# A spectral-filter and gated-MLP layer rewritten: one-instruction GELU, a stacked 64x32 FFT with trips through DRAM, and another order of work

## The chip, the cores and the metric

The kernel runs on one core of one Trainium2 chip. Times are device microseconds (us) of one execution. A quoted time is the median of several executions, with the lowest and highest behind it. Engines: PE is TensorE's matmul stream and PEld its weight loads, DVE is VectorE, ACT is ScalarE, POOL is GpSimd, SP is SyncE, which issues DMAs here (in the kernel before, ScalarE issues a part of them). An eviction is the copy of a matmul's result out of PSUM, where TensorE writes it. A DMA's landing is its end as the profile shows it. The chain of waits is the work that ended last, followed back from the end of the execution: at each step to what released it.

## The reference

```python
# x: (1, 2048, 576), hidden width Fh = 2304, everything in bfloat16
xn = layernorm(x)
# branch A: a spectral filter over both axes
s  = irfft2(rfft2(xn) * (w_r + 1j * w_i))
# branch B: a gated MLP that mixes over the 2048 rows
z  = gelu(xn @ w_in)                       # 2048 x 4608, the tanh form of GELU
z1, z2 = z[:, :2304], layernorm(z[:, 2304:])
g  = w_sp @ z2 + b_sp[:, None]             # w_sp: 2048 x 2048
out = x + s * silu((z1 * g) @ w_out)       # w_out: 2304 x 576
```

## The kernel before

It works in four stages: normalise all rows of x; compute z2 (for 16 row tiles) while the FFT of branch A runs between; mix over rows, one group of 128 hidden columns at a time (18 groups, all 2048 rows each); multiply by `w_out` and finish. Three parts matter here.

GELU was spelled out, two ScalarE passes and four VectorE passes for each tile:

```python
def gelu_from_psum(ph, nsz, dst, pp):                                    # L265
    nc.scalar.activation(out=hs, in_=ph, func=ACT.Identity)              # L267
    nc.vector.tensor_tensor(out=x2t, in0=hs, in1=hs, op=ALU.mult)        # L269
    nc.vector.tensor_scalar(out=x2t, in0=x2t, scalar1=GELU_K, scalar2=1.0, ...)   # L270
    nc.vector.tensor_tensor(out=ut, in0=x2t, in1=hs, op=ALU.mult)        # L273
    nc.scalar.activation(out=sg, in_=ut, func=ACT.Sigmoid, scale=GELU_S2)  # L275
    nc.vector.tensor_tensor(out=dst, in0=hs, in1=sg, op=ALU.mult)        # L276
```

(slices of the tiles are left out). The z2 loop (L476 to L493) makes each row of z2 with it, takes statistics, and stores the row to DRAM, from where the main loop loads it back by columns and normalises it.

The FFT over the 2048 rows was 128 x 16, with real and imaginary parts in separate matmuls and TensorE transposes between the steps. Four of its loops transpose; one of the two that also multiply, with matmuls of 128 columns:

```python
for lq in range(LQ):                                                     # L398, 37 times
    for c in range(2):
        nc.tensor.transpose(pt[:], Ev[:, c, lq, :], ident[:])
        nc.any.tensor_copy(out=dtt[:, c, :], in_=pt[:])
    nc.tensor.matmul(pvr[:], lhsT=H[:, 0, :], rhs=dtt[:, 0, :], start=True, stop=False)
    nc.tensor.matmul(pvr[:], lhsT=H[:, 2, :], rhs=dtt[:, 1, :], start=False, stop=True)
    nc.tensor.matmul(pvi[:], lhsT=H[:, 0, :], rhs=dtt[:, 1, :], start=True, stop=False)
    nc.tensor.matmul(pvi[:], lhsT=H[:, 1, :], rhs=dtt[:, 0, :], start=False, stop=True)
    nc.any.tensor_copy(...)   # two more evictions of 128x128
```

The main loop (L543 to L582) makes z1 for a group (L561, GELU), then multiplies `z2t` by all of `w_sp` (L571).

## Time and profile before

The kernel takes 760.86 us (759.58 to 761.64, 5 runs). The stages, read from the timeline and the groups by line:

| stretch, us | what runs | what bounds it |
|---|---|---|
| 0 to 36 | normalisation of x | VectorE and the loads |
| 36 to 187 | z2, with FFT steps between | VectorE |
| 187 to 348 | the rest of the FFT, alone | a chain of short matmuls and evictions |
| 348 to 676 | z1 and the mixing over rows | TensorE |
| 676 to 759 | load of `w_out`, output | TensorE, after a wait |

From parts 1 and 2 of the page of the kernel before. Each digit is the busy share of one fortieth of the span in tenths; PEclk is the granted TensorE clock in tenths.

```profile
PE 672.2 (89%) x3638; PEld 341.6 (45%) x3638; DVE 522.8 (69%) x1598; ACT 332.8 (44%) x900; POOL 15.7 (2%) x32
PE   3599977878795896797999999999999999989997
DVE  7779999998879533215987777777777778642322
PEclk9999999898556555598999999999999999999999
```

The 89% for TensorE hides three different limits (slices counted from 0). From slice 19 on PE is at 9 nearly throughout. In slices 3 to 8 DVE is at 9. In slices 10 to 16 no engine stays there, and the clock is at 5 or 6.

The busy time of each engine by stretch, kernel before. The columns after the stretch and its length are busy us and instructions of PE, PEld, DVE, ACT and POOL, then the granted clock, the DMA share and GB/s.

```profile
57.00:190.00 133.00, 110.99 (x578) 59.69 (x576) 128.07 (x403) 99.91 (x252) 0.42 (x2) 0.92 0.16 64
190.00:323.00 133.00, 104.23 (x608) 63.76 (x609) 72.68 (x219) 91.41 (x351) 7.19 (x4) 0.54 0.35 69
348.00:676.00 328.00, 328.00 (x1509) 148.18 (x1510) 253.25 (x736) 86.05 (x145) 3.08 (x15) 0.99 0.16 37
```

In the first line VectorE is busy 128 of 133 us: it is the bound. In the second no engine is busy throughout, and TensorE's 104 busy us are at a clock of 0.54. In the third TensorE is busy all 328 us. VectorE is busy 253 us there too, but nobody waits for it for long.

The GELU groups of the kernel before, by form. Columns: line, engine, operation, tiles, sizes, count, then busy us and mean ns of one.

```profile
L267 ACT ACTIVATE hs<-ph 128x512 bf16<-128x512 f32 x136 | 80.1, 598 | 205.9 <-PE ph L561 183.6 <-PE pf L285 10.0 <-DVE zrow L276 6.5
L269 DVE TENSOR_TENSOR x2t<-hs 128x512 bf16<-128x512 bf16 x136 | 56.2, 414 | 27.5 <-ACT hs L267 27.5
L270 DVE TENSOR_SCALAR x2t<-x2t 128x512 bf16<-128x512 bf16 x136 | 37.9, 288 | 0.8
L273 DVE TENSOR_TENSOR ut<-x2t,hs 128x512 bf16<-128x512 bf16 x136 | 55.7, 419 | 0.1
L275 ACT ACTIVATE sg<-ut 128x512 bf16<-128x512 bf16 x136 | 84.0, 630 | 61.1 <-DVE ut L273 36.0 <-DMA wb<-in_B_w_in_dram 24.5
L276 DVE TENSOR_TENSOR zrow<-hs,sg 128x512 bf16<-128x512 bf16 x64 | 26.4, 417 | 3.1 <-ACT sg L275 3.0
```

A 512-wide tile costs VectorE 414 + 288 + 419 + 417 = 1,538 ns. TensorE needs five matmuls of 216 ns for it, 1,080 ns. So in the z2 loop VectorE must set the pace.

A piece of the chain of waits of the kernel before (start us, us, what):

```profile
429.91 11.22 PE pg L571 x52
```

11.22 us by 52 is 215.8 ns for a 512-wide matmul in a dense stream.

### The profile page before, as it was taken

How to read it: one execution, taken by the hardware profiler on the slowest of the kernel's cores; microseconds unless marked ns; L12 is line 12 of the kernel's file. 1: busy time of each engine (PE TensorE's matmuls, PEld its weight loads, DVE VectorE, ACT ScalarE, POOL GpSimd, SP SyncE). 2: the span in 40 equal slices, each digit the busy share in tenths (PEclk: the TensorE clock that was granted, in tenths of full speed). 3: DMA queues.
4: the chain of work that ended last, by engine and by line, in shares of the span. 5: the costliest groups of instructions: out<-in, count | busy, mean ns of one | idle time of the engine just before them, and what ended most of it. 6: DMA issues, size and time to landing. Idle time of an engine off the chain costs nothing.

```text
span 759.1 us, 10654 instructions
## 1 busy us (share of the span) xinstructions
PE 672.2 (89%) x3638; PEld 341.6 (45%) x3638; DVE 522.8 (69%) x1598; ACT 332.8 (44%) x900; POOL 15.7 (2%) x32
## 2 busy tenths in 40 slices
PE   3599977878795896797999999999999999989997
PEld 1276533333562563353444444444444444434553
DVE  7779999998879533215987777777777778642322
ACT  3447787677774677734222222222222223202222
POOL 2000000000000110000000000000000000000000
PEclk9999999898556555598999999999999999999999
DMA  7091111111598000034311111111111210025331
GB/s 265 18 315 71 63 63 62 64 62 63 124 217 135 1 1 0 1 104 115 84 38 35 37 36 36 36 37 36 36 37 44 48 43 1 0 90 169 95 109 56
DMA packets 104374, 54.08 MB, mean 71 GB/s; under 512 B 84160, under 2 KB 101184, under 8 KB 104192
## 3 DMA queue, kind: packets, MB, share of 16 engines
q10 hardware_dynamic: 61040, 29.36, 13.6%
q1 hardware_dynamic: 43280, 24.05, 12.1%
q8 instruction: 28, 0.46, 0.2%
q14 instruction: 26, 0.21, 0.1%
HBM read 30.85 MB, written 14.16 MB: 59 GB/s over the span
## 4 chain that ended last, share of the span: by engine, by line
PE 70%; DVE 17%; ACT 8%; issue 2%; DMA 2%; ACTq 0%; DVEq 0%
PE pg L571 33%; PE ph L561 11%; PE py L600 9%; PE ph L485 5%; DVE stats L490 4%; PE py L461 3%; DVE zrow L276 2%; DVE x2t L269 2%; DVE ut L273 2%; PE pt L435 2%; ACT G L438 2%; DVE x2t L270 1%; ACT dtt L406 1%; PE pvr L410 1%; PE pxr L346 1%
## 5 line engine op out<-in xcount | busy, mean ns | idle before, releaser
L571 PE MATMUL pg<-WSPT,z2t 128*128 128x512 bf16 x1152 | 253.9, 379 | 0.0
L267 ACT ACTIVATE hs<-ph 128x512 bf16<-128x512 f32 (+1 forms) x152 | 85.6, 577 | 205.9 <-PE ph L561 183.6
L571 PEld LDWEIGHTS <-z2t 128*128 128x128 bf16 x1152 | 112.7, 98 | 136.0
L275 ACT ACTIVATE sg<-ut 128x512 bf16<-128x512 bf16 (+1 forms) x152 | 89.0, 607 | 61.3 <-DVE ut L273 36.2
L485 PE MATMUL ph<-WIN,xnT 128*128 128x512 bf16 (+1 forms) x400 | 96.1, 389 | 7.0 <-ACT hs L267 6.4
L561 PE MATMUL ph<-xnT,wb 128*128 128x512 bf16 x360 | 85.3, 387 | 4.9 <-DMA wb<-in_B_w_in_dram 4.9
L577 DVE TENSOR_TENSOR BUF<-pg,z1T 128x512 bf16<-128x512 f32 x72 | 49.5, 688 | 44.5 <-PE pg L571 43.7
L269 DVE TENSOR_TENSOR x2t<-hs 128x512 bf16<-128x512 bf16 (+1 forms) x152 | 60.0, 400 | 27.5 <-ACT hs L267 27.5
L600 PE MATMUL py<-WOUT,BUF 128*128 128x512 bf16 (+1 forms) x576 | 73.0, 289 | 3.9 <-DMA WOUT<-in_B_w_out_dram 3.7
L554 DVE TENSOR_SCALAR z2t<-z2t,RSTD,NMR 128x128 bf16<-128x128 bf16 x288 | 74.0, 312 | 1.8 <-DMA z2t<-z2n_d 1.5
L485 PEld LDWEIGHTS <-xnT 128*128 128x128 bf16 x400 | 40.8, 104 | 52.0 <-issue 26.6
L273 DVE TENSOR_TENSOR ut<-x2t,hs 128x512 bf16<-128x512 bf16 (+1 forms) x152 | 59.0, 405 | 0.1
L561 PEld LDWEIGHTS <-wb 128*128 128x128 bf16 x360 | 35.8, 100 | 48.9 <-issue 7.9
L600 PEld LDWEIGHTS <-BUF 128*128 128x128 bf16 x576 | 37.4, 99 | 40.0 <-issue 6.3
L490 DVE BATCH_NORM_STATS2 stats<-zrow 128x6 f32<-128x384 bf16 x96 | 48.2, 548 | 0.0
L606 DVE TENSOR_TENSOR g<-hx,sgm 128x576 bf16<-128x576 bf16 x16 | 7.3, 458 | 55.1 <-ACT sgm L604 44.2
L603 ACT ACTIVATE hx<-py 128x512 bf16<-128x512 f32 (+1 forms) x32 | 13.2, 414 | 66.7 <-PE py L600 46.1
L270 DVE TENSOR_SCALAR x2t<-x2t 128x512 bf16<-128x512 bf16 (+1 forms) x152 | 40.1, 281 | 0.8
L197 PE MATMUL pt<-ident,xn 128*128 128x128 bf16 (+1 forms) x80 | 14.2, 296 | 21.4 <-DVE xn L192 18.9
L276 DVE TENSOR_TENSOR zrow<-hs,sg 128x512 bf16<-128x512 bf16 (+1 forms) x80 | 29.7, 391 | 3.1 <-ACT sg L275 3.0
L276 DVE TENSOR_TENSOR z1T<-hs,sg 128x512 bf16<-128x512 bf16 x72 | 30.1, 419 | 1.9 <-ACT sg L275 1.5
L580 DVE TENSOR_TENSOR BUF<-BUF,zb 128x512 bf16<-128x512 bf16 x72 | 29.0, 422 | 1.3
(131 smaller groups left out, 736.0 us busy)
## 6 DMA issues: line engine op xcount, KB each, us to landing
z2t<-z2n_d ACTq DMA_DIRECT2D x18, 512.0 KB, 3.9
z2n_d<-zrow ACTq DMA_DIRECT2D x8, 576.0 KB, 2.8
z2n_d<-zrow SPq DMA_DIRECT2D x8, 576.0 KB, 2.8
sspec_d<-srow ACTq DMA_DIRECT2D x16, 144.0 KB, 1.8
wb<-in_B_w_in_dram ACTq DMA_DIRECT2D x72, 32.0 KB, 1.9
GA<-c_ga ACTq DMA_DIRECT2D x1, 1536.0 KB, 8.9
WOUT<-in_B_w_out_dram SPq DMA_DIRECT2D x9, 144.0 KB, 3.7
WOUT<-in_B_w_out_dram ACTq DMA_DIRECT2D x9, 144.0 KB, 3.7
```

Of the source, the lines that this page charges most:

```text
L267: nc.scalar.activation(out=hs[:, 0:nsz], in_=ph[:, 0:nsz], func=ACT.Identity)
L269: nc.vector.tensor_tensor(out=x2t[:, 0:nsz], in0=hs[:, 0:nsz], in1=hs[:, 0:nsz], op=ALU.mult)
L273: nc.vector.tensor_tensor(out=ut[:, 0:nsz], in0=x2t[:, 0:nsz], in1=hs[:, 0:nsz], op=ALU.mult)
L275: nc.scalar.activation(out=sg[:, 0:nsz], in_=ut[:, 0:nsz], func=ACT.Sigmoid, scale=GELU_S2)
L276: nc.vector.tensor_tensor(out=dst, in0=hs[:, 0:nsz], in1=sg[:, 0:nsz], op=ALU.mult)
L485: nc.tensor.matmul(ph[:, 0:nsz], lhsT=xnT[:, ks, m * P:(m + 1) * P], rhs=WIN2[:, ks, f0:f0 + nsz], start=(ks == 0), stop=(ks == DKS - 1))
L490: nc.vector.bn_stats(out=stats2[:, ci, :], in_=zrow[:, c0:c0 + cs])
L554: nc.vector.tensor_scalar(out=z2t[:, m, :], in0=z2t[:, m, :], scalar1=RSTD2[:, m, :], scalar2=NMR2[:, m, :], op0=ALU.mult, op1=ALU.add)
L561: nc.tensor.matmul(ph[:, 0:nsz], lhsT=wb[:, ks, :], rhs=xnT[:, ks, nb * 512: nb * 512 + nsz], start=(ks == 0), stop=(ks == DKS - 1))
L571: nc.tensor.matmul(pg[:, 0:nsz], lhsT=z2t[:, ks, :], rhs=WSPT[:, ks, nb * 512: nb * 512 + nsz], start=(ks == 0), stop=(ks == MT - 1))
L577: nc.vector.tensor_tensor(out=dst, in0=pg[:, 0:nsz].rearrange("p (a u) -> p a u", u=P), in1=z1T[:, nb * 512: nb * 512 + nsz].rearrange("p ...
L600: nc.tensor.matmul(py[:, 0:dn], lhsT=BUF[:, m, fi * P:(fi + 1) * P], rhs=WOUT[:, fi, d0:d0 + dn], start=(fi == 0), stop=(fi == FT - 1))
```

## The change

The intent was to take VectorE's work out of the z2 stage, to shrink the FFT and hide it among the z2 matmuls, and to keep TensorE dense to the end. The kernel was rewritten whole (643 lines became 460). Its core, with cuts marked:

```diff
 # GELU of z2 (z1 in the same way)
-nc.scalar.activation(out=hs, in_=ph, func=ACT.Identity)
-... four VectorE operations and ACT.Sigmoid
+nc.scalar.activation(out=Z2[m][:, n*ZC:(n+1)*ZC], in_=ph[:], func=ACT.Gelu_apprx_tanh)   # L330, ZC = 384
+nc.vector.bn_stats(out=st[:, n, :], in_=Z2[m][:, n*ZC:(n+1)*ZC])                         # L331
 ...
 # z2 stays in SBUF, normalised there at once
-dq().dma_start(out=z2n_d[m*P:(m+1)*P, :], in_=zrow[:])
+nc.gpsimd.tensor_tensor(out=rs[:], in0=ve[:], in1=mhalf[:, 0:n], op=ALU.pow)             # L209
+nc.vector.tensor_scalar(out=Z2[m][:], in0=Z2[m][:], scalar1=mv[:, 0, 0:1], scalar2=rs[:],
+                        op0=ALU.subtract, op1=ALU.mult)                                  # L334
 ...
 # FFT over rows: 64 x 32, real and imaginary parts stacked on the partitions, 289 columns wide (128 in p4);
 # what was a TensorE transpose is a store to DRAM and a load in another order (three trips)
-nc.tensor.transpose(pt[:], BPv[:, c, lq, :, :], ident[:])   # and three more loops of transposes
-nc.tensor.matmul(pxr[:], lhsT=M16[:, 0, :], rhs=tt[:, 0, :], ...)
+nc.sync.dma_start(out=Adw[m], in_=sg)                                                    # L243, 16 stores
+nc.sync.dma_start(out=ain, in_=rowv(Ad)[:, ch*8*L:(ch+1)*8*L])                           # L250, 4 loads
+nc.tensor.matmul(pa[:, j, 0:L], lhsT=G1[:, ch*8+i+j, :], rhs=av[:, i+j, :], ...)         # L257
+nc.sync.dma_start(out=rowv(Bd)[:, ...], in_=bs)                                          # L262
+... p23: load, L282 matmuls, L284 product with the filter, L288 matmuls, store to Ed
+... p4: load, L301 matmuls, L303 eviction into V
 ...
 # program order; the scheduler fills waits of the FFT with z2
+for ch in range(4): p1(ch)
+for ch in range(4): p23(ch)
+for ch in range(4): p4(ch)
+for m in range(MT): z2(m)        # 480 matmuls of 384 columns
+for j in range(MT): p5(j)        # inverse DFT over columns, stores to Yd
 ...
 # main loop by quarters of the rows; output of a quarter inside the next
-for fi in range(FT):             # all 2048 rows of a column group
+steps = [(q, fi) for q in range(NQ) for fi in range(FT)]
+for k in range(NK): z1(k + 1); main(k); ... outm(q - 1, i)
```

## The prediction

> **What bounds the kernel now.** The per-stretch table and the chain of waits show three stages. From 348 to 676 us TensorE is the bound: fully busy at clock 1.0, 56 of the 128x512 matmuls taking 12.09 us in the chain, 216 ns each; 1,512 of them need 326 us. From 680 to 754 us the output runs as densely. The slack lies before 348 us. Row normalisation takes 36 us. From 57 to 190 us VectorE is the bound (17 to 19 busy us in every 19): each GELU tile costs it four operations (414, 288, 419 and 417 ns in the groups by form) and ScalarE two. From 190 to 323 us the FFT's short 128-wide matmuls and evictions run alone, at a TensorE clock of 0.5 to 0.7.
>
> **What the change does.**
> - GELU becomes one ScalarE activation: about 219 us of VectorE work (60+40+59+60) and one of two ScalarE passes go. The Trainium skill, ScalarE: Activation LUTs, says that time per element is the same for every function, so I cost it like the 598 ns eviction.
> - The FFT becomes 64x32 with real and imaginary parts stacked; matmuls are 289 wide, and the transposes between steps become three trips through DRAM (about 2.4 MB each way).
> - z2 stays in SBUF. Its 480 matmuls of 384 columns fill the waits of the FFT steps.
> - The main loop goes by row quarters: the same 1,512 wide matmuls, with 576 output matmuls of 288 in between.
>
> **Cost.** 215.9 ns for a 512-wide matmul agrees with the Trainium skill, TensorE: Matmul & The Clock Gate (back-to-back issue gap). Estimates from its formula: 384 wide 162 ns, 289 wide 123 ns. TensorE in all: mixing 249, z1 78, output 71, z2 78, FFT about 55, transposes 9: 540 us, against 672 busy now.
>
> By stage (estimates from the durations above):
> - To the last forward-DFT matmul: 45 us. statistics of ten row tiles stand ahead on VectorE, so TensorE starts at about 13 us and then needs 29.
> - z2 with the FFT steps: TensorE 102 us; VectorE about 115: 96 statistics at 502 ns (48), 16 normalisations at about 1 us, 32 spectrum products at about 0.76 us (24), evictions 21, aggregates 5. With short waits for DRAM and for POOL's inverse square root: 122 us.
> - Inverse DFT over columns, mixed with the first main steps: 22 us.
> - Rest of main loop, output: 387 us.
> - Last eviction and store: 6 us.
>
> Sum 582; 8 more for cold clock after waits: 590 us. Nearly all of the 170 us saved comes from before the main loop, some 10 from the output, none from the main loop.
>
> **What would show it right.** TensorE fully busy at clock 1.0 for about 385 us to the end, 216 ns per wide matmul; first mixing matmul near 180 us; VectorE at 90% or more from 50 to 165 us; TensorE busy about 540 us; no half-clock stretch over 10 us.
>
> **What would make it wrong.** POOL's power operation (not in the trace before) could take microseconds and stall VectorE 16 times. The DRAM trips may cost more than the 6 to 8 us of z2 work put ahead of each: all DMAs share one queue. The middle could run at half clock. Slab transposes (5.3 us to land, 2.5 us issue each) may delay quarters.
>
> Range (8 in 10): 560 to 630 us. Chances: faster by over 2% 0.97, within 2% 0.02, slower 0.01.

## The result, and the profile after

The kernel after takes 584.43 us (580.81 to 586.38, 9 runs), the kernel before 761.18 us in the same rounds (16 runs). The ratio is 0.7674, with a 95% interval of 0.7658 to 0.7691. Ratios here are the mean time of one kernel's runs over that of the other's of the same rounds, so they are not quite the ratios of the medians.

From parts 1 and 2 of the page of the kernel after:

```profile
PE 545.5 (94%) x3128; PEld 299.5 (51%) x3128; DVE 243.4 (42%) x468; ACT 145.9 (25%) x258; POOL 23.7 (4%) x69
PE   0896999998979999999999999999999999999996
DVE  5703799989876322222422222332222233222223
PEclk9999999999979999999999999999999999999999
```

VectorE's busy time fell from 523 to 243 us, TensorE's from 672 to 546. The stretch at a clock of 5 is gone.

The busy time of each engine by stretch, kernel after (columns as before):

```profile
15.00:45.00 30.00, 27.02 (x230) 20.32 (x231) 12.08 (x36) 17.86 (x26) 3.93 (x11) 1.00 0.82 216
45.00:60.00 15.00, 10.15 (x55) 5.61 (x54) 5.90 (x11) 7.54 (x14) 0.74 (x2) 0.89 0.70 242
60.00:165.00 105.00, 97.80 (x673) 60.25 (x671) 95.22 (x165) 57.43 (x113) 11.19 (x30) 1.00 0.57 159
165.00:190.00 25.00, 22.84 (x127) 13.06 (x128) 15.62 (x38) 6.99 (x16) 0.74 (x2) 0.86 0.41 102
190.00:576.00 386.00, 386.00 (x2039) 199.33 (x2037) 104.72 (x189) 50.98 (x84) 0.00 (x0) 1.00 0.27 66
```

From 190 to 576 us TensorE is dense at clock 1.0. In the z2 and FFT stretch (60 to 165 us) TensorE and VectorE are both near full: 97.8 and 95.2 of 105 us.

The groups of the kernel after that answer to the GELU groups:

```profile
L330 ACT ACTIVATE z<-ph 128x384 bf16<-128x384 f32 x96 | 46.7, 491 | 40.2 <-PE ph L328 39.9
L383 ACT ACTIVATE AR<-ph 128x512 bf16<-128x512 f32 x72 | 43.0, 597 | 261.5 <-PE ph L381 261.5
L331 DVE BATCH_NORM_STATS2 st<-z 128x6 f32<-128x384 bf16 x96 | 48.0, 543 | 11.8 <-ACT z L330 11.6
L334 DVE TENSOR_SCALAR z<-z,mv,rs 128x2304 bf16<-128x2304 bf16 x16 | 14.1, 879 | 7.9 <-POOL rs L209 7.9
```

GELU of a 512-wide tile takes 597 ns on ScalarE, and the plain eviction took 598 ns before. That agrees with the Trainium skill, ScalarE: Activation LUTs (ACT is a hardware spline evaluator), which says that throughput does not depend on the function. What VectorE still has of z2 is statistics and one normalisation for each row tile.

Pieces of the chain of waits of the kernel after:

```profile
39.78 8.09 DMA Ad<-AR
...
52.07 4.34 DMA AR<-Ad
...
123.90 5.50 DMA Ed<-AR
129.42 4.02 DMA AR<-Ed
133.49 0.63 PE pa L301 x8
134.15 13.67 DVE AR L303 x12
147.81 1.39 DVE st L331 x3
...
190.57 3.45 PE pg L389 x16
```

All three trips through DRAM stand in the chain: the first with 8.09 us of store and 4.34 us of load, the third with 5.50 and 4.02. After the third the chain is on VectorE (12 evictions of 1.14 us, then statistics) until 167 us, and on TensorE from there: 3.45 us by 16 is 215.6 ns for each matmul.

Where did 177 us go? The main loop's 1,512 wide matmuls need about 326 us in both kernels (1,512 times 0.2157). Before, the main loop took 328 us and the output with its wait 83. After, the output's 576 matmuls take 17.64 us for each of four quarters, 71 us, and the tail is 5.5. So the output gave about 7 us, the main loop about 2, and the part ahead of the main loop gave the rest: 348 us became 581.5 - 326 - 76, about 179.

### The profile page after: what moved, and what is told of

Same layout as the page of the kernel before. It is cut to its first block, busy times and chain, and to the rows that moved or that the text cites. A ratio compares the mean times of both kernels' runs of the same rounds, so it can differ in the third digit from the quotient of the medians.

```text
span 581.5 us, 7782 instructions
## 1 busy us (share of the span) xinstructions
PE 545.5 (94%) x3128; PEld 299.5 (51%) x3128; DVE 243.4 (42%) x468; ACT 145.9 (25%) x258; POOL 23.7 (4%) x69
## 4 chain that ended last, share of the span: by engine, by line
PE 79%; DVE 8%; DMA 8%; ACT 2%; issue 1%; POOL 1%; SPq 0%; ACTq 0%; DVEq 0%; POOLq 0%
PE pg L389 43%; PE ph L381 13%; PE po L403 12%; PE ph L328 5%; DMA Ad<-AR 3%; DVE AR L303 2%; PE pa L312 2%; DVE st L331 2%; PE pb L288 1%; DMA AR<-in_A_x_dram 1%; PE pa L239 1%; ACT AR L242 1%; DMA Ed<-AR 1%; DVE st L218 1%; DVE z L334 1%
## 5 line engine op out<-in xcount | busy, mean ns | idle before, releaser
L389 PE MATMUL pg<-AR,z 128*128 128x512 bf16 x1152 | 262.2, 379 | 0.0
L389 PEld LDWEIGHTS <-z 128*128 128x128 bf16 x1152 | 112.9, 98 | 134.6 <-issue 0.6
L392 DVE TENSOR_TENSOR AR<-pg,AR 128x512 bf16<-128x512 f32 x72 | 49.8, 692 | 226.5 <-PE pg L389 226.5
L383 ACT ACTIVATE AR<-ph 128x512 bf16<-128x512 f32 x72 | 43.0, 597 | 261.5 <-PE ph L381 261.5
L328 PE MATMUL ph<-RW,xnT 128*128 128x384 bf16 x480 | 88.3, 329 | 2.8 <-ACT z L330 2.8
L381 PE MATMUL ph<-xnT,AR 128*128 128x512 bf16 x360 | 90.1, 380 | 0.0
L403 PE MATMUL po<-AR,RW 128*128 128x288 bf16 x576 | 71.2, 286 | 0.0
L403 PEld LDWEIGHTS <-RW 128*128 128x128 bf16 x576 | 56.4, 98 | 14.9
L330 ACT ACTIVATE z<-ph 128x384 bf16<-128x384 f32 x96 | 46.7, 491 | 40.2 <-PE ph L328 39.9
L331 DVE BATCH_NORM_STATS2 st<-z 128x6 f32<-128x384 bf16 x96 | 48.0, 543 | 11.8 <-ACT z L330 11.6
## 6 DMA issues: line engine op xcount, KB each, us to landing
Ad<-AR SPq DMA_DIRECT2D x16, 144.5 KB, 3.8
AR<-in_A_w_r_dram SPq DMA_DIRECT2D x16, 144.5 KB, 3.3
AR<-in_A_w_i_dram SPq DMA_DIRECT2D x16, 144.5 KB, 3.7
```

The costliest lines, as they stand in the source:

```text
L328: nc.tensor.matmul(ph[:], lhsT=xnT[:, m, ks, :], rhs=WIN2[:, ks, n * ZC:(n + 1) * ZC], start=(ks == 0), stop=(ks == KS - 1))
L330: nc.scalar.activation(out=Z2[m][:, n * ZC:(n + 1) * ZC], in_=ph[:], func=ACT.Gelu_apprx_tanh)
L331: nc.vector.bn_stats(out=st[:, n, :], in_=Z2[m][:, n * ZC:(n + 1) * ZC])
L381: nc.tensor.matmul(ph[:].rearrange("p (a t) -> p a t", a=4), lhsT=wb[:, ks, (fi % WG) * P:(fi % WG + 1) * P], rhs=xnT[:, 4 * q:4 * q + 4, ...
L383: nc.scalar.activation(out=Z1T[k % 3], in_=ph[:], func=ACT.Gelu_apprx_tanh)
L389: nc.tensor.matmul(pg[:], lhsT=Z2[m][:, fi * P:(fi + 1) * P], rhs=SLAB[q % 2][:, m, :], start=(m == 0), stop=(m == MT - 1))
```

## The experiments

My theory was: (a) VectorE's GELU work was the bound of the z2 stage, and taking it away there is necessary for the gain but not sufficient, because the FFT tail at half clock stays; (b) the FFT becomes cheap only because its waits are filled with z2 matmuls; (c) GELU in the main loop was worth nothing. The rivals were: the whole gain is GELU; or the whole gain is the smaller FFT, and neither GELU nor the filling matters much.

Each run was timed beside the kernel before on the same chip. The medians of the kernel before were 761.25 to 761.72 us.

### GELU alone, in the kernel before (before_gelu)

```diff
 def gelu_from_psum(ph, nsz, dst, pp):
-    ... six operations
+    nc.scalar.activation(out=dst, in_=ph[:, 0:nsz], func=ACT.Gelu_apprx_tanh)
```

> The kernel before, with the one-instruction GELU alone. My theory: the saving before the main loop has two parts that hide each other. The GELU takes about 117 us of VectorE work out of the stretch to 190 us, but TensorE itself was busy 111 us of the 133 us from 57 to 190, and the FFT tail from 190 to 323 us at half clock stays. So the gain is small: 15 to 45 us, total 715 to 745 us; the main loop (348 to 676 us before) keeps its 328 us. Rival: the GELU is what the whole change gains, and the FFT rewrite adds little: then this run comes to 640 us or less.

Measured: 718.35 us (717.68 to 719.65), ratio 0.9436. The rival that says GELU is everything falls. Busy time by stretch of this kernel:

```profile
57.00:190.00 133.00, 121.24 (x813) 74.06 (x825) 89.20 (x258) 91.56 (x259) 0.42 (x2) 1.00 0.41 113
190.00:285.00 95.00, 69.95 (x416) 41.00 (x417) 39.96 (x116) 61.44 (x220) 7.19 (x4) 0.59 0.16 33
310.00:632.00 322.00, 320.38 (x1463) 145.50 (x1490) 160.97 (x435) 41.10 (x69) 3.18 (x15) 1.00 0.16 36
```

The z2 matmuls end at 155.8 us, where they ended at 187.4. The FFT tail from 190 to 285 us still runs at a clock of 0.59. The mixing lasts from 309.7 to 631.5 us, 321.8 us, and it lasted 321.8 us before as well (354.6 to 676.4), although VectorE has 92 us less to do there (253 to 161). So this change of 11 lines gave 43 us: about 32 in the z2 stage, and 13 in the tail between it and the mixing (167.2 us before, 153.9 now), less 2 lost in the output.

### The old GELU in z2 of the kernel after (z2_oldgelu)

```diff
-nc.scalar.activation(out=Z2[m][:, n*ZC:(n+1)*ZC], in_=ph[:], func=ACT.Gelu_apprx_tanh)
+gelu_parts(Z2[m][:, n*ZC:(n+1)*ZC], ph[:], ZC)      # the six operations of before
```

> The changed kernel, with the old six-operation GELU in the 96 z2 tiles only. My theory: the stretch from 45 to 160 us is bound by VectorE, so 96 tiles x about 1.24 us (four operations of 384 columns, scaled from 414+288+419+417 ns at 512) = 119 us come on top almost in full: 690 to 710 us. Rival: the stretch is set by TensorE and by the DRAM trips, and VectorE has room: then less than 40 us more.

Measured: 685.97 us (685.72 to 687.9), 102 us more than the kernel after. The theory holds, and the rival that GELU does not matter falls. The time fell a little below the range I gave, because VectorE had some room before: the four operations took 123 us of it in this run (32.7 + 24.2 + 32.9 + 33.5), and of the 120 us from 45 to 165 us it had been idle 19 in the kernel after. The difference, 104, is close to the 102 measured. Busy time by stretch of this kernel:

```profile
60.00:270.00 210.00, 135.65 (x732) 71.88 (x732) 195.09 (x532) 100.96 (x206) 11.36 (x30) 0.91 0.43 117
```

Over a window of 210 us, where the kernel after had done with the stage in 105, VectorE is busy 93% (195.09 us), and TensorE only 65%. ScalarE, which has its second pass again, is busy 101 us, so it is not the bound. The same operations that were worth 43 us in the old kernel are worth 102 us in the new one, in the z2 tiles alone. The worth of a part depends on what else bounds its stage.

### The old GELU in the main loop of the kernel after (z1_oldgelu)

```diff
-nc.scalar.activation(out=Z1T[k % 3], in_=ph[:], func=ACT.Gelu_apprx_tanh)
+gelu_parts(Z1T[k % 3], ph[:], 512)
```

> The changed kernel, with the old GELU in the 72 z1 tiles of the main loop only. My theory: VectorE is busy 27 of 100 us there; 111 us more over 385 us are hidden behind TensorE, so the time stays within 5 us of 584 (only the first steps, mixed with the inverse DFT, can show something). Rival: the longer chain from matmul to product delays the main steps: 20 us more or above.

Measured: 583.21 us (582.4 to 585.52), the same as the kernel after (583.31 and 584.43). Busy time of this kernel in the main loop, to be read against the last line of the table by stretch of the kernel after:

```profile
190.00:576.00 386.00, 384.42 (x2009) 199.19 (x2036) 212.23 (x467) 94.30 (x153) 0.00 (x0) 1.00 0.26 66
```

VectorE's work doubled there, from 105 to 212 us, and nothing changed. TensorE stayed busy throughout.

### No z2 matmuls in the waits of the FFT (no_fill)

```diff
 for ch in range(4):
     p4(ch)
+tc.strict_bb_all_engine_barrier()
 for m in range(MT):
     z2(m)
```

> The changed kernel with a barrier of all engines between the FFT steps (up to the step before the column DFT) and the z2 matmuls, so that z2 can't fill the waits. My theory: each of the three DRAM trips then stands open for 8 to 10 us, and the product step runs at the pace of its chain (matmul, two products, matmul, eviction, about 3 us a pair): some 100 us for the FFT and then 80 us for z2 in place of 115 us for both: 640 to 665 us. Rival: the overlap is worth only the three trips: 10 to 30 us more.

Measured: 644.63 us (643.84 to 645.01), about 60 us more than the kernel after. The theory holds. Busy time by stretch of this kernel, then TensorE's waits from 76 to 120 us:

```profile
45.00:150.00 105.00, 54.67 (x241) 27.29 (x242) 43.81 (x54) 19.24 (x30) 0.77 (x2) 0.51 0.52 158
76.00:120.00 44.00, 27.05 (x92) 10.60 (x92) 21.39 (x30) 9.14 (x14) 0.00 (x0) 0.50 0.60 161
150.00:228.00 78.00, 78.00 (x483) 47.06 (x481) 64.65 (x128) 46.91 (x96) 11.90 (x32) 1.00 0.19 42
```

```profile
PE pb L288 <- DVE AR L284: 16.4, 30, 0.9
PE pa L282 <- DMA AR<-Bd: 8.8, 1, 8.8
```

The windows are cut at round times; by the first and last matmuls the FFT runs from 45 to 144 us, at a clock of about 0.5, and z2 from 146 to 225 us at 1.0. Run one after the other they take 180 us. Run together they took 115 us (45 to 160). TensorE waits 11.5, 8.8 and 8.0 us for the three loads, where it waited 2.1, 0.8 and 2.9 us in the kernel after; so the three trips alone, the rival's claim, are about 22 of the 60 us. The stacked FFT is short in matmuls but not in time: alone, it waits for three trips and for VectorE's product at each step, and TensorE's clock stays at half. The one wait above 1 us in the second stretch is that for the load of the second trip, and it ended at 76.5 us, right at the beginning. After it the clock stayed at 0.50 although no single wait was longer than 0.9 us.

### The branch taken out, in both kernels (after_nofft, before_nofft)

```diff
-... all of the branch's steps
+nc.gpsimd.memset(zt[:], 0.0)          # and its result stored as zeros
```

Both give a wrong result (the relative error is 0.0276 in each).

> The changed kernel without the spectral branch (zeros are written in its place, so the result is wrong on purpose). My theory: z2 then starts right behind the first row tiles and is bound by TensorE (480 matmuls of about 163 ns, 78 us); 15 + 80 + 397 + 6 = about 498 us, 490 to 515; so the branch costs about 85 us of the 584. Rival: the branch hides fully behind z2 and the start: 550 us or more.

> The kernel before without its spectral branch (zeros, wrong on purpose). My theory: normalisation 36 us, then z2 bound by VectorE with the old GELU (about 10.6 us a row tile, 170 us), then the unchanged 410 to 420 us: 610 to 640 us; so the branch cost about 135 us of the 761, and the rewrite of the branch saves about 50 of the 177 us, the rest is GELU and order. Rival: the branch was the main cost: 560 us or less.

Measured: 513.27 us (512.91 to 514.26) for the kernel after without the branch, and 630.23 us (628.82 to 631.61) for the kernel before without it. So taking the branch out saves 584 - 513, about 70 us, in the kernel after; I expected 85, but z2 began at 30.5 us and not at 15, since the transposes of the normalised rows stand ahead of it (TensorE waited 18.8 us for ScalarE there). It saves 761 - 630, about 131 us, in the kernel before; I expected 135. By these two runs, about 61 of the 177 us saved (131 - 70) come from the branch's rewrite with its filling, and about 117 (630 - 513) from everything else: GELU, z2 kept in SBUF, the order of the main loop and the output. No run splits the 117 further with the branch taken out.

The 131 is a lower bound for the branch in the kernel before. Without the FFT tail, the load of `w_sp` has nothing to hide under. A wait of TensorE in before_nofft (us in total, times, longest), which the kernel before doesn't have:

```profile
PE pg L380 <- DMA WSPT<-in_B_w_sp_dram: 19.6, 2, 17.0
```

ScalarE also waited 8.7 us there for the branch's constants, whose loads this run kept. If both waits had been hidden, the 61 would be up to about 28 us larger and the 117 as much smaller (an estimate; not tested).

### More staging for the forward DFT's stores (stg7)

```diff
+STG0 = STG + [reg("TT", i*2*L, 2*L) for i in range(4)]
-sg = STG[m % 3].rearrange("p (c l) -> p c l", c=2)
+sg = STG0[m % 7].rearrange("p (c l) -> p c l", c=2)
```

> The changed kernel with seven staging tiles in place of three for the forward DFT's trip to DRAM (four of them in a region free until the product step). The trace shows ScalarE held for 7.0 us by stores that had not landed, and TensorE short of z2 evictions behind it from 45 to 57 us. My theory: the staging tiles are the cause; the last eviction moves from 48 to about 45 us, 3 to 6 us less in all. Rival: the DMA engines (0.8 to 0.9 busy to 45 us) set the pace; the wait only moves to the first load of the next step: within 2 us of the base.

Measured: 581.16 us (579.35 to 583.15), and the kernel after 583.31 us (582.49 to 584.14), named after_again.

> The changed kernel once more, as the base of the three runs beside it: 580 to 587 us.

A gain of about 2 us, with ranges that overlap: the rival was closer. The waits say why. First the kernel after, then this one, from 15 to 70 us:

```profile
ACT AR L242 <- DMA Ad<-AR: 7.0, 4, 4.2
```

```profile
PE pa L258 <- DMA AR<-Ad: 5.2, 1, 5.2
```

ScalarE no longer waits for its stores, and TensorE now waits 5.2 us for the load at the other end of the same trip (2.1 us before). The last eviction starts 6.5 us earlier (42.2 us, it was 48.7), the next step only 2.5 us (54.0, it was 56.5). Most of the wait moved; it did not end.

### Fourteen evictions moved from VectorE to ScalarE (relief)

```diff
-if i % 4 == 0:          # p1: half of the evictions on ScalarE
+if True:                # all of them
-nc.vector.tensor_copy(out=V[...], in_=pa[...])
+if (ch*NLC + lc) % 2 == 0:
+    nc.vector.tensor_copy(out=vo, in_=vi)
+else:
+    nc.scalar.activation(out=vo, in_=vi, func=ACT.Identity)
```

> The changed kernel with 14 evictions moved from VectorE to ScalarE: half of the twelve 1,024-wide ones before the column DFT (1.2 us each) and all of the first column step's (0.75 us each), about 10 us of VectorE work. My theory: VectorE sets the end of the z2 stretch (the chain of waits runs on it from 134 to 166 us), TensorE then waits 7.5 us for it: 5 to 9 us less. Rival: TensorE and DRAM waits set the stretch, VectorE only trails: within 2 us of the base.

Measured: 579.55 us (579.18 to 581.02), about 4 us less than the kernel after. The direction is the theory's, the size a bit less than I expected. VectorE is a bound of the stage, but not the only one.

### Both, and four more evictions on ScalarE (best1)

```diff
+if m < 4:
+    nc.scalar.activation(out=xnT[:, m, :, :], in_=pt[:], func=ACT.Identity)
+else:
     nc.vector.tensor_copy(out=xnT[:, m, :, :], in_=pt[:])
```

> Both of the above, and the first four transposed row tiles evicted by ScalarE, so that they don't stand behind statistics on VectorE (TensorE waited 3.9 us for the first one). My theory: the three add up, 9 to 17 us less than the base. Rival: all of it is held by DMA in the start; less than 4 us.

Measured: 576.31 us (571.92 to 576.85), 7 us less than the kernel after, where I expected 9 to 17. TensorE still waited 5.1 us for the loads of the first trip.

### Constants loaded later (late2)

```diff
 for ch in range(4):
     p23(ch)
+    if ch == 0:
+        nc.gpsimd.tensor_copy(out=G4[:, 0, 0:2], in_=TT[0][:, 0, 0, 0:2])       # a small write that the load must wait for
+        nc.gpsimd.tensor_copy(out=CESO[:, 0, 0, 0:2], in_=TT[0][:, 0, 0, 0:2])
+        ... the two loads, moved here from ahead of the loop; and one such write for the bias load
```

> best1 (576.31 us) with the loads of the inverse DFT's constants (1.0 MB and 0.43 MB) made to wait until the first spectrum product, and the bias load until the inverse column DFT. In best1 those 1.4 MB stand in the one DMA queue among the last stores of the forward DFT, whose median from issue to landing was 6.7 us. Theory: the forward trip waits for the queue. Then the last stores land in about 2.5 to 4 us, the first matmul of the next step starts 2 to 4 us earlier (51.95 us in best1), and the time falls by 2 to 4 us, to 572 to 574. Rival: the wait is the trip's own latency (store, then read) and the queue had room; then the landing stays at 6 us or more and the time is within 1.5 us of best1's, 575 to 578.

Measured: 571.0 us (570.0 to 573.3), 5 us less than best1 by the medians and 4 by the means. The two were timed in different calls; their ratios to the kernel before, 0.7554 (0.7528 to 0.758) and 0.7501 (0.748 to 0.7522), do not overlap. The theory holds: the first trip was waiting for the loads of constants. Whether it waited for its place in the queue or for DMA engines busy with them, the run does not tell. DMA issues from 20 to 60 us (size, median us from issue to landing) and the first matmul that needs the trip (the times behind the comma are its first and last start), first best1, then late2:

```profile
Ad<-AR SPq DMA_DIRECT2D x13, 144.5 KB, 5.9
L261 PE MATMUL pa<-AR x32: 283/288/448, 51.9 to 65.0; 128*128 128x289 bf16 x32
```

```profile
Ad<-AR SPq DMA_DIRECT2D x13, 144.5 KB, 3.9
L261 PE MATMUL pa<-AR x32: 283/287/290, 47.5 to 59.2; 128*128 128x289 bf16 x32
```

The same stores land 2 us sooner, and the next step starts 4.4 us sooner. This version is the best: it beats the kernel before by 190 us (ratio 0.7501, 0.748 to 0.7522) and the kernel after by 12 to 13 us (584.43 and 583.31).

### Five staging tiles for the inverse DFT's stores (best2c)

```diff
+YST = [t[:, 0:D] for t in STG] + YIN
-y = STG[j % 3][:, 0:D]
+y = YST[j % 5]
```

> late2 with five staging tiles in place of three for the stores of the inverse DFT's rows (VectorE waited 8.0 us in 11 pieces for those stores in best1). Theory: VectorE no longer waits there, TensorE's weight loads (6.3 us in 13 waits for VectorE there) come earlier, and the time falls by another 2 to 3 us. Rival: that stretch is bound by VectorE's and ScalarE's own evictions, so the waits move and the time stays within 1 us of late2's.

Measured: 573.0 us (570.7 to 574.09), no gain over late2. VectorE no longer waited for those stores, and from 150 to 180 us TensorE was busy 29.15 us instead of 27.88. But a new wait stands behind it. A piece of the chain of waits of this kernel:

```profile
179.74 11.52 DMA AR<-in_B_w_in_dram
```

A slice of z1's weights (384 KB) came after 11.5 us; the 2.6 MB load of `w_out` was issued right ahead of it, at 178.8 us (in late2 it was issued 6.6 us ahead of it, at 175.7). TensorE waited 3.1 us for the slice. So neither theory holds as I wrote it: the stretch did get denser, by 1.3 us, and this wait took that back. That the order of the queue is its cause is read from the trace, not shown: I did not run a version that repairs it.

## Why the prediction was right

I predicted 590 us, 560 to 630; measured were 584.43. Point by point:

- **What bounds the kernel.** Right in each stage. before_gelu shows that VectorE was the bound of the z2 stage of the kernel before, that the FFT tail stays near half clock without that work, and that the mixing lasts 321.8 us either way; z1_oldgelu shows that VectorE is no bound in the main loop of the kernel after.
- **Where the gain lies.** I wrote that nearly all of it comes from before the main loop, some 10 us from the output and none from the main loop. The trace has about 168, 7 and 2.
- **Forward DFT, 45 us.** The last group began at 44.9 us. The first matmul came at 15.9 us, not 13: TensorE stood 3.9 us for a copy that was queued on VectorE behind statistics. The estimate of the work had room for it.
- **z2 with the FFT, 122 us.** It took about 115 to 120 us (45 to 160 or 165). The size was right with some luck: from 45 to 165 us VectorE was busy 101 us, 14 less than its sum, and TensorE 108, 6 more than its own, so the waits were longer than the 7 us allowed on top of VectorE's 115.
- **Inverse DFT, 22 us.** It took about 27 (160 to 187): VectorE waited 3.0 us for its stores and TensorE 3.5 us for VectorE. This term was too small. The terms sum to 582 us and the span is 581.5, partly because this error and that of the z2 term cancel; the 8 us added for a cold clock were not needed.
- **Rest of the main loop and output, 387 us; tail, 6.** Measured 389 and 5.5.
- **Matmul times.** The estimates from the Trainium skill, TensorE: Matmul & The Clock Gate (Back-to-back issue gap), were 162 ns for 384 columns and 123 for 289. The chain has 0.49 us for three 384-wide matmuls, 163 ns each, and 1.49 us for twelve 289-wide ones, 124 ns each. TensorE's busy time was 545.5 us against 540.
- **VectorE at 90% or more from 50 to 165 us.** Half wrong. From 60 to 165 it was 91% (95.2 of 105), but from 45 to 60 only 39%, since the first trip through DRAM held the work back there.
- **First mixing matmul near 180 us.** It came at about 169, mixed with the inverse DFT; dense mixing began at 187.
- **The dangers.** POOL's power operation took 551 ns for 128x1 and made VectorE wait 7.9 us in all, not microseconds each time. The three loads at the ends of the trips cost TensorE 2.1, 0.8 and 2.9 us, since z2 stood ready. The half clock did not come for as long as 10 us (the mean clock was 0.89 from 45 to 60 us and 0.77 from 165 to 180).

What the prediction left without a cost is the first trip. It named the danger (all DMAs share one queue), but gave this trip no more than a short wait. In the kernel after, the store that was issued at 39.78 us, right behind a 1.0 MB load of constants, took 8.09 us to land. late2 shows, against best1, that moving such loads makes a store land 2 us sooner (the median) and the next step start 4.4 us sooner. These two figures belong to best1, where the median from 20 to 60 us was 5.9 us; in the kernel after it was 3.7 us and in stg7 4.1, so they are no measure of what the queue cost there.

## What to carry to other kernels

Cost a changed operation in the stage where it runs and against the engine that bounds that stage: the same GELU was worth 43 us in one schedule, 102 us in another and nothing in the main loop. A chain of small dependent steps is cheap only if independent matmuls fill its waits, because alone it also ran at half clock (180 us one after the other, 115 together). Taking a part out also uncovers the loads that it was hiding, so read the waits of such a run before the difference is taken as the part's cost. Read a wait at both ends of a DMA: where more buffers only move the wait to the load, look at what else stands in the queue, and move what is not needed yet behind it.

## What the Trainium skill lacked or had wrong

- **TensorE: Matmul & The Clock Gate, Back-to-back issue gap.** The page says that a stream of weight loads and matmuls sustains about 131 ns for each matmul at N=512, and that its formula (N/2.4 + 2.5) gives too much there. In these runs such a dense stream took 215.8 ns for each in the kernel before and 215.6 ns after, and 163 ns at N=384: the formula, which the prediction used, was right and the sustained figure was not reached. At N=128, 8 matmuls in 0.63 us (79 ns each) agree with the page's 81.
- **TensorE: Matmul & The Clock Gate, Why this matters for your kernels.** The page advises to have no idle gap above about 3 us, against drops of throughput in mid-kernel; another row asks for 4 us of unbroken work to reach the full clock. The run no_fill agrees with the two rows together and shows that the first alone is not enough once the clock is down: from 76 to 120 us the clock was 0.50, with no wait above 0.9 us after one that ended at 76.5 us, TensorE being counted busy 27 of 44 us. In the kernel before it was counted busy 17.94 of 19 us from 266 to 285 us, with short matmuls, and the clock was 0.50 too. So the busy share of the profile does not foretell the clock, and no run here shows which stream would have lifted it.
- **ScalarE: Activation LUTs, Table sets.** The table only says that the tanh form of GELU is separate from `gelu_and_others`. In the kernel after, Identity, this GELU and Tanh ran with two table loads in all (1,283 ns each, which agrees with the page's section What ACT_TABLE_LOAD costs), none of them between GELU and Tanh.
- **GPSIMD Engine Reference, Elementwise — side-by-side cycle accounting.** The page works out an addition of 2048 columns; no page has the cost of the power operation, or of an instruction on one column. Here the power took 551 ns for 128x1 and about 1,010 ns for 128x4; a multiplication of 128x4 took 198 ns (the profile's spans on POOL are rough).
- **DMA: Bandwidth & Descriptors, Anatomy of one DMA — SWDGE (gpsimd) path.** Its fit for the GpSimd path (2.0 us and bytes by 436 GB/s) would give an estimate of 2.3 us for a store of 144.5 KB. Such stores, issued from SP, took a median of 5.9 us with large loads of constants among them (best1) and 3.9 us without (late2); no page states how to cost a small store in a queue of large loads.
